# Down products of the middle pairs: weights standing and 512 tokens moving, output turned by VectorE

## The chip, the cores and the metric

The kernel runs on one core of one Trainium2 chip. The metric is the device time of one execution in microseconds (us). A core has TensorE for matrix products, VectorE and ScalarE for elementwise work, GpSimd, and SyncE, which here only issues DMAs. SBUF is the working memory with 128 partitions. Products go to PSUM, which has eight banks; a bank holds 512 float32 values on each of the 128 partitions. Each engine takes its instructions in the order in which the program gives them, and waits for other engines through semaphores.

## The reference

The program is a delta-rule attention followed by a dense layer pair.

- Attention: batch 4, 8 heads, 768 steps, head width 48. With normalized keys, step t gives `y[t] = q[t] @ state`, and then `state += beta[t] * outer(k[t], v[t] - k[t] @ state)`.
- The results of the heads stand beside each other: `x` has 3,072 tokens of 384 values.
- Dense part: `h = x @ w_in` (384 to 2,048); `g = h` where `h >= 1`, 0 where `h <= -1`, `(h + 1)^2 / 4` between; `out = g @ w_out` (2,048 to 384).

Inputs and output are float32.

## The kernel before, in words

The 768 steps are cut into 12 chunks of 64. Two chunks are a pair `G` (0 to 5); a pair has 512 tokens (4 batches, 2 chunks, 64 steps). For a pair, the dense part runs in 16 items, one for each 128 of the 2,048 middle columns (`items`, L614 to L621; pair 0 has its first columns split by chunk). While the dense items of pair G run, the attention of pair G+1 runs in pieces between them.

**An item.** `up` (L630) makes `h` (128 middle columns by 512 tokens) with nine products: three blocks of 128 rows of `x`, and three passes for each (`PASSES`: high part times high part, high times low, low times high, which together give float32 accuracy). ScalarE and VectorE make `g` from it (L776, L788, L789, maximum at L791), and `rest` (L753) splits it into `ghi` and `glo`, each a tile of 128 by 512 with two buffers. `down` (L639) multiplies `g` with `w_out`: for each of four blocks of 128 tokens, the tokens stand as weights and 384 columns of `WT` move, in three passes: twelve products an item. They accumulate over the 16 items in four banks, `o0` to `o3` (`oacc`, 128 tokens by 384). A down runs two items after its up (`LAG`), so the last down of pair G stands in item 1 of pair G+1, behind that item's up, and the first down of pair G+1 in item 2.

**The store.** After the last down of a pair, `store` (L653) copies the four banks to SBUF on ScalarE, and SyncE issues two DMAs for each bank, each of 64 tokens with 384 contiguous values. In the last pair ScalarE and VectorE take turns at the copies, and the very last DMA is issued by ScalarE.

**The order.** The schedule is written out by hand. Each item has two places for other work, at half-item numbers: `at(pe, G, t, ...)` puts a piece of products at item t of pair G (whole t: between up and down; half t: after down), and `at(fill, G, t, ...)` puts steps of other engines there. In the main loop (L765 to L794) an item gives, in this order: the late evictions of the piece before, `rest` of the item before, up, the first activation, the piece at t, the fills at t, the evictions of that piece, down and possibly store, two activations, the piece at t + 0.5, the maximum, the fills at t + 0.5. Pieces at half places are evicted at the start of the next item.

**The pieces of a pair** (`plan`, L674) for the chunks a and b of the next pair, in the middle pairs 1 to 4: `chain_r` 2.5, `gram_q(a)` 4.5, `gram_q(b)` 6, three merges (`merge32`, L385) at 8.5, 9 and 11, `gram_k` 9.5 and 12 (pairs 1 to 3), and the chain `chain_u`, `chain_y`, `chain_d`, `chain_r`, `chain_u`, `chain_y`, `chain_d` from 10 to 15. Each takes one or two banks from `acc()` (L65): from item 6 of pair 0 on, this is the name `ch` with two buffers, taken in turn. So the banks are: two `h`, two `ch`, four `o`. `gram_q` is evicted by VectorE with three masked multiplications (L237), the merges by ScalarE (L399 to L406).

**The solve.** A triangular system for each pair is solved on VectorE in 30 steps of two instructions (L325, L327), spread by a cost sum over the items from 2.5 or 1.5 before a pair's start to its item 6 or so; then four steps turn the result (L333 to L338), which the merges read. The steps are fills, so they stand on VectorE's queue between the glo subtraction and the maximum of the items.

**DMA.** SyncE's queue is in order too: it holds the loads of keys, queries and values for later pairs (`load_k`, `load_q`, `load_kv`), the moves of `chain_y` (L484) and the stores. `load_kv(b + 2)` stands right behind a pair's stores.

Of the kernel before, what the change touches and what calls it, by code (L numbers as in the profile page):

```python
# [7 lines left out]
F32 = mybir.dt.float32  # L8
# [5 lines left out]
C = 64  # L14
NP = 4
D = 48
CT = 2
NV = CT * NP
DM = 384
# [11 lines left out]
def delta_rule_moe(ctx: ExitStack, tc: tile.TileContext, kqa, kqb, kv, beta, w, out):  # L31
# [185 lines left out]
    def gram_q(g):  # L217

        x, b_ = Q[g], banks(C)
        for j in range(H):  # L220
            for e, f in quarters():
                r, o = slice(f * C, f * C + D), other(e, f) * C
                nc.tensor.matmul(b_[e][o:o + C, j], K[g][r, e * H + j, :], x[r, (1 - f, 1)[e], e * H + j, :], start=True, stop=True)  # L223

        def moved():
            for o in range(2):
                yield x[o * C:o * C + C, o, 0:H], b_[0][o * C:o * C + C], slice(o * C, o * C + C)
            yield x[:, 0, H:NU], b_[1], slice(0, P)

        def evict():  # L230
            def raw():
                for a, b, r in moved():
                    nc.scalar.copy(out=a, in_=b)

            def masks(copied=False):
                for a, b, r in moved():
                    nc.vector.tensor_tensor(out=a, in0=a if copied else b, in1=mask[r, None, :].broadcast_to([r.stop - r.start, H, C]), op=ALU.mult)  # L237
                    yield
            return (raw, masks(True)) if g < 2 else lambda: run(masks())
        return evict  # L240
# [389 lines left out]
    def up(G, f, bs):  # L630
        h = ps.tile([P, 2 * NB], F32, name="h", bufs=2)
        n = 0
        for k in range(3):
            for x, y in PASSES:
                nc.tensor.matmul(h[:, cols(bs)], WT[f][:, 0, x, k * P:(k + 1) * P], XB[G][:, y, k, cols(bs)], start=(n == 0), stop=(n == 8))  # L635
                n += 1
        return h

    def down(G, f, bs):  # L639
        ghi, glo = gs.pop((G, f, bs))  # L640
        for b in bs:
            left[G, b] -= 1
            for k in (2 * b, 2 * b + 1):
                if (G, k) not in oacc:
                    oacc[G, k] = ps.tile([P, DM], F32, name=f"o{k}")
                    new = True
                else:
                    new = False
                for n, (x, y) in enumerate(PASSES):
                    nc.tensor.matmul(oacc[G, k], (ghi, glo)[x][:, k * P:(k + 1) * P], WT[f][:, 1, y, :],  # L650
                                     start=(new and n == 0), stop=(left[G, b] == 0 and n == 2))

    def store(G, b):  # L653
        o = sb.tile([P, 2, DM], F32, name="wx", bufs=2)
        for k in (2 * b, 2 * b + 1):
            (nc.scalar.copy, nc.vector.tensor_copy)[k % 2 if G == NS - 1 else 0](out=o[:, k % 2], in_=oacc[G, k])
            for j in range(CT):
                (nc.scalar if G == NS - 1 and k + j == TT else nc.sync).dma_start(out=out.rearrange("(b n t) m -> n b t m", b=CB, t=C)[2 * G + b, k % 2 * CT + j], in_=o[j * C:j * C + C, k % 2])

    pe, fill = {}, {}  # L660

    def at(where, G, t, *x):
        where.setdefault(2 * first[G] + int(round(2 * t)), []).extend(x)
# [5 lines left out]
    def chain(G, t, a):  # L669
        for j, f, g in ((0, chain_u, a), (0.5, chain_y, a), (1.5, chain_d, a), (2.5, chain_r, a + 1), (3.5, chain_u, a + 1), (4, chain_y, a + 1), (5, chain_d, a + 1)):  # L670
            if (f, g) != (chain_d, ntot - 1):
                at(pe, G, t + j, lambda f=f, g=g: f(g))

    def plan(G):  # L674

        a, b = 2 * G + 2, 2 * G + 3
        if G == NS - 1:
            return
        va, vb = scale_v(a), scale_v(b)
        if G == 0:  # L680
            for j, f in ((0, merge16_b), (0.5, chain_r), (1, lambda g: merge32(g, None, True)), (2, lambda g: merge32(None, g)), (3, chain_u), (4, chain_y), (5, chain_d)):
                at(pe, G, j, lambda f=f: f(1))
            back = restore()
            at(fill, G, 0, (sv[1], 2))
            at(fill, G, 1, (load_k, b), (weight_loads, 7, 9), (load_q, a), (weight_loads, 9, 10), (load_kv, a), (weight_loads, 10, 13))
            at(fill, G, 1.5, (back, 1))
            at(fill, G, 2.5, (back, 1), (raws[1][1], 9))
            for j, n in enumerate((2, 2, 3)):
                at(fill, G, 3.5 + j, (early[0], n))
            at(fill, G, 6.5, (early[1], 1))  # L690
            at(fill, G, 7, (early[1], 9))
            at(fill, G, 4.5, (load_q, b), (weight_loads, 13, 14))
            at(fill, G, 5.5, (load_kv, b), (weight_loads, 14, 15))
            at(fill, G, 8, (load_k, a + 2), (weight_loads, 15, FT))
            for j in range(2):
                at(fill, G, 6 + j / 2, (va, 1))
                at(fill, G, 11.5 + j / 2, (vb, 1))
            at(pe, G, 6, lambda: gram_q(a))
            at(pe, G, 7, lambda: chain_r(a))
            at(pe, G, 11, lambda: gram_q(b))  # L700
            for j, f in ((8, merge16_a), (9.5, merge16_b)):
                for g in range(2):
                    at(pe, G, j + g / 2, lambda f=f, g=g: f(g))
            M = 12.5
            last = FT + HALF
        else:
            so, un = solves.pop(G)
            at(fill, G, 0.5, (va, 1))
            at(fill, G, 1, (va, 1))
            at(pe, G, 2.5, lambda: chain_r(a))  # L710
            at(pe, G, 4.5, lambda: gram_q(a))
            at(pe, G, 6, lambda: gram_q(b))
            cost, hs = 0, 0
            t, n = (-2.5, 19) if G == 1 else (-1.5, 17)
            for j in range(1, 31):
                at(fill, G, t + hs / 2, (so, 1))
                cost += j * (31 - j) + 150
                hs = int(cost / 9461 * n)
            for j, t in enumerate((7, 7.5, 8, 8)):
                at(fill, G, t, (un, 1))  # L720
            at(fill, G, 9, (vb, 1))
            at(fill, G, 9.5, (vb, 1))
            M = 8.5
            last = 16
        for j, x in ((0, (0, None)), (0.5, (1, 0)), (2.5, (None, 1))):
            at(pe, G, M + j, lambda x=x: merge32(*x))
        chain(G, M + 1.5, a)
        if G < NS - 2:
            if G:
                at(fill, G, 6.5, (load_k, a + 2))  # L730
            at(fill, G, M + 0.5, (load_k, b + 2, (nc.sync, nc.sync), True))
            at(pe, G, M + 1, lambda: gram_k(a + 2))
            at(pe, G, M + 3.5, lambda: gram_k(b + 2))
            lane_steps(G, M + 2, lanes(G + 2), 2.5, 3, 3.5, 4)
            solves[G + 1] = solve_whole(), unlanes_whole()
            at(fill, G, M + 3, (load_q, a + 2))
            at(fill, G, M + 5, (load_k, b + 2))
            at(fill, G, M + 6.5, (load_q, b + 2))
            at(fill, G, last + 0.5, (load_kv, a + 2))
            at(fill, G, last + 1.5, (load_kv, b + 2))  # L740
# [24 lines left out]
    for n, item in enumerate(items):  # L765
        at_, c = 2 * n, cols(item[2])
        finish(late)
        if last:
            rest(*last)
            ready.append(last[0])  # L770
        if at_ == 2 * HALF:
            spare.clear()
        h = up(*item)

        s = sb.tile([P, 2 * NB], F32, name="s", bufs=2)
        relu(s[:, c], h[:, c], mid, -0.5)  # L776
        evicts = products(*pe.pop(at_, []))
        run(wu, 3 if n == 0 else 1)
        fills(at_)
        finish(evicts)  # L780
        run(wu, 2 if n < HALF else 1)
        if len(ready) == LAG:
            x = ready.pop(0)
            down(*x)
            for b in x[2]:
                if left[x[0], b] == 0:
                    store(x[0], b)
        relu(s[:, c], s[:, c], one, -1.0)  # L788
        nc.scalar.activation(out=s[:, c], in_=s[:, c], func=AF.Square)  # L789
        late = products(*pe.pop(at_ + 1, []))  # L790
        nc.vector.tensor_tensor(out=s[:, c], in0=h[:, c], in1=s[:, c], op=ALU.max)  # L791
        run(wu, 2)
        fills(at_ + 1)
        last = item, s  # L794
# [3 lines left out]
    for b in range(2):  # L798
        gs[G, FT - 1, (b,)] = gs[G, FT - 1, (0, 1)]
        down(G, FT - 1, (b,))  # L800
        store(G, b)

# [1 line left out]
def layouts(q, k, v, beta, moe_w_in, moe_w_out):  # L804
# [43 lines left out]
```

## Time and profile before

| what | value |
|---|---|
| median of three runs | 622.01 us (621.1 to 622.45) |
| the profiled execution | 620.85 us |
| its span, first to last instruction | 619.1 us |
| mean granted TensorE clock | 0.943 |
| TensorE products busy | 583.6 us, 94% |
| VectorE busy | 409.3 us, 66% |
| ScalarE busy | 393.9 us, 64% |
| up products with 512 columns | 810, 402 ns mean |
| down products with 384 columns | 1,152, 339 to 344 ns mean |

The times of single products overlap, since TensorE is pipelined; how fast they follow each other is read from their starts. The rows of the profile have the start in us, the length, the engine (PE is TensorE, PEld its weight loads, DVE is VectorE, ACT is ScalarE, SPq the DMA queue of SyncE), the line, the operation, the tiles written and read, the shape and the count, and in brackets the idle time before it with what ended it.

### The profile page before, as it was taken

How to read it: one execution, taken by the hardware profiler on the slowest of the kernel's cores; microseconds unless marked ns; L12 is line 12 of the kernel's file. 1: busy time of each engine (PE TensorE's matmuls, PEld its weight loads, DVE VectorE, ACT ScalarE, POOL GpSimd, SP SyncE). 2: the span in 40 equal slices, each digit the busy share in tenths (PEclk: the TensorE clock that was granted, in tenths of full speed). 3: DMA queues.
4: the chain of work that ended last, by engine and by line, in shares of the span. 5: the costliest groups of instructions: out<-in, count | busy, mean ns of one | idle time of the engine just before them, and what ended most of it. 6: DMA issues, size and time to landing. Idle time of an engine off the chain costs nothing.

```text
span 619.1 us, 21754 instructions
## 1 busy us (share of the span) xinstructions
PE 583.6 (94%) x9562; PEld 511.5 (83%) x9562; DVE 409.3 (66%) x848; ACT 393.9 (64%) x685; POOL 29.8 (5%) x62
## 2 busy tenths in 40 slices
PE   7977967799999999999999999999999999999996
PEld 7966956688888888888888888888888888889995
DVE  4989899972379873379973489954489945333332
ACT  3436775649667569656578646587647586666663
POOL 5110000010010000020000020000020000000000
PEclk9556697999999999999999999999999999999999
DMA  5672756200124210214210224110124000020002
GB/s 141 197 244 71 233 196 202 88 4 3 42 61 119 74 31 3 69 31 125 72 30 8 65 53 119 54 31 24 49 71 124 1 4 16 12 54 1 0 1 51
DMA packets 32831, 42.97 MB, mean 69 GB/s; under 512 B 7152, under 2 KB 27440, under 8 KB 32736
## 3 DMA queue, kind: packets, MB, share of 16 engines
q1 hardware_dynamic: 31600, 39.43, 22.6%
q10 hardware_dynamic: 880, 2.07, 1.0%
q8 instruction: 75, 1.23, 0.8%
q0 software_dynamic: 256, 0.08, 0.1%
q14 instruction: 20, 0.16, 0.1%
HBM read 34.47 MB, written 4.72 MB: 63 GB/s over the span
## 4 chain that ended last, share of the span: by engine, by line
PE 70%; ACT 11%; DVE 9%; SPq 3%; DMA 3%; issue 2%; DVEq 0%; ACTq 0%
PE o L650 27%; PE h L635 27%; PE ch L452 3%; ACT XT L406 2%; ACT GG L404 2%; PE ch L414 2%; ACT s L762 2%; PE ch L223 2%; PE ch L430 1%; ACT XT L399 1%; PE ch L496 1%; PE o L583 1%; PE ch L375 1%; ACT s L789 1%; SPq L484 1%
## 5 line engine op out<-in xcount | busy, mean ns | idle before, releaser
L635 PE MATMUL h<-xb,wt 128*128 128x512 f32 (+1 forms) x918 | 229.1, 395 | 9.1 <-DMA xb<-wt 8.1
L635 PEld LDWEIGHTS h<-xb,wt 128*128 128x128 f32 x918 | 166.8, 195 | 43.2 <-DVE xb L183 4.4
L650 PE MATMUL o<-wt,ghi 128*128 128x384 f32 x768 | 202.1, 344 | 0.1
L791 DVE TENSOR_TENSOR s<-h,s 128x512 f32<-128x512 f32 (+1 forms) x102 | 66.8, 655 | 124.3 <-ACT s L789 123.8
L650 PEld LDWEIGHTS o<-wt,ghi 128*128 128x128 f32 x768 | 137.8, 189 | 7.5 <-issue 0.5
L757 ACT CAST ghi<-s 128x512 fp32r<-128x512 f32 (+1 forms) x102 | 60.8, 597 | 110.4 <-DVE s L791 86.3
L650 PE MATMUL o<-wt,glo 128*128 128x384 f32 x384 | 130.3, 339 | 0.4 <-DVE glo L758 0.3
L762 ACT ACTIVATE s<-h,half 128x512 f32<-128x512 f32 (+1 forms) x102 | 67.5, 662 | 44.6 <-PE h L635 43.7
L758 DVE TENSOR_TENSOR glo<-s,ghi 128x512 fp32r<-128x512 f32 (+1 forms) x102 | 66.6, 653 | 34.9 <-ACT ghi L757 34.8
L650 PEld LDWEIGHTS o<-wt,glo 128*128 128x128 f32 x384 | 72.7, 189 | 1.0 <-DVE glo L758 1.0
L762 ACT ACTIVATE s<-s,one 128x512 f32<-128x512 f32 (+1 forms) x102 | 71.7, 703 | 2.4
L789 ACT ACTIVATE s<-s 128x512 f32<-128x512 f32 (+1 forms) x102 | 61.9, 607 | 3.2
L325 DVE TENSOR_TENSOR pr<-A 128x30 f32<-128x30 f32 (+14 forms) x120 | 39.3, 328 | 6.2 <-POOL A L296 4.5
L327 DVE TENSOR_TENSOR A<-A,pr 128x30 f32<-128x30 f32 (+14 forms) x120 | 39.9, 332 | 4.4
L452 PEld LDWEIGHTS ch<-Q,SU 64*64 64x64 f32 (+1 forms) x1008 | 22.1, 135 | 4.3 <-ACT ghi L757 1.5
L452 PE MATMUL ch<-Q,SU 64*64 64x64 f32 (+1 forms) x1008 | 24.3, 222 | 0.7 <-ACT SU L434 0.7
L237 DVE TENSOR_TENSOR Q<-ch,mask 64x512 f32<-64x512 f32 (+1 forms) x30 | 20.6, 688 | 0.4
L296 POOL TENSOR_SCALAR_AFFINE_SELECT A<-A 128x1024 f32<-128x1024 f32 x4 | 5.1, 1263 | 311.9 <-DMA xb<-X 258.1
L404 ACT ACTIVATE GG<-ch 32x512 f32<-32x512 f32 x22 | 13.0, 589 | 10.6 <-PE ch L392 10.3
L414 PEld LDWEIGHTS ch<-SU,K 48*64 48x64 f32 x672 | 13.2, 147 | 6.5 <-issue 4.6
L414 PE MATMUL ch<-SU,K 48*64 48x48 f32 x672 | 14.9, 232 | 3.7 <-DVE Q L237 3.7
L179 ACT ACTIVATE xb<-wt 128x768 f32<-128x768 f32 x16 | 14.5, 914 | 5.1 <-DVE wt L191 3.6
(150 smaller groups left out, 621.8 us busy)
## 6 DMA issues: line engine op xcount, KB each, us to landing
wt<-in_w_dram SPq DMA_DIRECT2D x14, 768.0 KB, 5.4
out_dram<-wx SPq DMA_DIRECT2D x47, 96.0 KB, 2.2
KV<-in_kv_dram SPq DMA_DIRECT2D x36, 96.0 KB, 2.5
KV<-in_kv_dram SPq DMA_DIRECT2D x72, 48.0 KB, 2.4
KV<-in_kv_dram SPq DMA_DIRECT2D x12, 192.0 KB, 2.7
xb<-X SPq DMA_DIRECT2D x60, 32.0 KB, 2.0
K<-in_kqb_dram SPq DMA_DIRECT2D x12, 128.0 KB, 2.7
Q<-in_kqb_dram SPq DMA_DIRECT2D x12, 128.0 KB, 2.7
```

The costliest lines, as they stand in the source:

```text
L325: nc.vector.tensor_tensor(out=pr, in0=A[:, 0:n, j:j + 1].broadcast_to([P, n, m]), in1=A[:, j:j + 1, j + 1:32].broadcast_to([P, n, m]), op= ...
L327: nc.vector.tensor_tensor(out=A[:, 0:n, j + 1:32], in0=A[:, 0:n, j + 1:32], in1=pr, op=ALU.add)
L404: nc.scalar.mul(out=GG[r:r + 32, ga, :, 0:32], in_=y1[r:r + 32], mul=-1.0)
L414: nc.tensor.matmul(b_[f][o:o + C, j], K[g][r, k, :], SU[r, (1 - f, 1)[e], k, :], start=True, stop=True)
L452: nc.tensor.matmul(yy[i][o * C:o * C + C, e, p], SF[rows, u:u + C], w_[rows, x, k, :], **how)
L635: nc.tensor.matmul(h[:, cols(bs)], WT[f][:, 0, x, k * P:(k + 1) * P], XB[G][:, y, k, cols(bs)], start=(n == 0), stop=(n == 8))
L650: nc.tensor.matmul(oacc[G, k], (ghi, glo)[x][:, k * P:(k + 1) * P], WT[f][:, 1, y, :], start=(new and n == 0), stop=(left[G, b] == 0 and n ...
L757: nc.scalar.copy(out=ghi[:, c], in_=s[:, c])
L758: nc.vector.tensor_tensor(out=glo[:, c], in0=s[:, c], in1=ghi[:, c], op=ALU.subtract)
L762: nc.scalar.activation(out=out, in_=in_, func=AF.Relu, bias=bias, scale=scale)
L789: nc.scalar.activation(out=s[:, c], in_=s[:, c], func=AF.Square)
L791: nc.vector.tensor_tensor(out=s[:, c], in0=h[:, c], in1=s[:, c], op=ALU.max)
```

## The change

1. In pairs 1 to 4, `down_across` takes the place of `down`: the weights stand (`WT[f][:, 1, y, k::3]`, every third of 384 columns, 128 of them), and all 512 tokens of `ghi` or `glo` move. Nine products an item; the result has 128 output columns by 512 tokens in each of three banks, `o0` to `o2`. `k::3` gives bank k the columns k, k+3, and so on.
2. `store_across` turns it on VectorE: six transposes in blocks of 32 by 32, from 128x256 of PSUM to SBUF with a step of three elements, so that three banks interleave to rows of 96 contiguous values. Then SyncE issues 16 DMAs for each pair, each of 32 partitions with four runs of 96 values. ScalarE's four copies for each of these pairs go.
3. The bank `o3`, free in the middle pairs, becomes a third one for the pieces, from item 2 of pair 1 on.
4. In pairs 1 to 4, `gram_q(b)` moves from 6 to 8.5, behind the first merge there, and the third merge from 11 to 10.5, ahead of `chain_y`.
5. The last pair keeps `down`. Its stores are made by `store_last`: copies by ScalarE and VectorE in turn as before, the first half of each bank's tokens sent by SyncE, the second by ScalarE.

```diff
+    def down_across(G, f, bs):
+        g = gs.pop((G, f, bs))
+        for b in bs:
+            left[G, b] -= 1
+        for k in range(3):
+            if f == 0:
+                oacc[G, k] = ps.tile([P, 2 * NB], F32, name=f"o{k}")
+            for n, (x, y) in enumerate(PASSES):
+                nc.tensor.matmul(oacc[G, k], WT[f][:, 1, y, k::3], g[x],
+                                 start=(f == 0 and n == 0), stop=(f == FT - 1 and n == 2))
+
+    def store_across(G):
+        o = [sb.tile([P, CT, TT, 32, 3], F32, name="wx", bufs=2) for _ in range(2)]
+        for k in range(3):
+            for x in range(2):
+                nc.vector.transpose(out=o[x][:, :, :, :, k].rearrange("p e (b h) d -> p b e h d", b=2),
+                                    in_=oacc[G, k].rearrange("p (b x n) -> p x b n", b=2, x=2)[:, x].rearrange("p b (e h d) -> p b e h d", e=CT, h=2))
+        for x in range(2):
+            for e in range(CT):
+                for i in range(4):
+                    nc.sync.dma_start(out=out.rearrange("(e n t) (i m) -> e i t n m", e=CB, t=32, i=4)[2 * x + e, i, :, 4 * G:4 * G + 4],
+                                      in_=o[x][32 * i:32 * i + 32, e].rearrange("p n d k -> p n (d k)"))
+
     def store(G, b):
         o = sb.tile([P, 2, DM], F32, name="wx", bufs=2)
         for k in (2 * b, 2 * b + 1):
-            (nc.scalar.copy, nc.vector.tensor_copy)[k % 2 if G == NS - 1 else 0](out=o[:, k % 2], in_=oacc[G, k])
+            nc.scalar.copy(out=o[:, k % 2], in_=oacc[G, k])
             for j in range(CT):
-                (nc.scalar if G == NS - 1 and k + j == TT else nc.sync).dma_start(out=out.rearrange("(b n t) m -> n b t m", b=CB, t=C)[2 * G + b, k % 2 * CT + j], in_=o[j * C:j * C + C, k % 2])
+                send(G, k, j, o, nc.sync)
+
+    def send(G, k, j, o, q):
+        q.dma_start(out=out.rearrange("(b n t) m -> n b t m", b=CB, t=C)[2 * G + k // 2, k % 2 * CT + j], in_=o[j * C:j * C + C, k % 2])
+
+    def store_last(G):
+        o = [sb.tile([P, 2, DM], F32, name="wx", bufs=2) for _ in range(2)]
+        for k in range(TT + 1):
+            if k < TT:
+                (nc.scalar.copy, nc.vector.tensor_copy)[k % 2](out=o[k // 2][:, k % 2], in_=oacc[G, k])
+                send(G, k, 0, o[k // 2], nc.sync)
+            for x in ((0,), (), (1,), (), (2, 3))[k]:
+                send(G, x, 1, o[x // 2], nc.scalar)
...
-            at(pe, G, 6, lambda: gram_q(b))
...
-        for j, x in ((0, (0, None)), (0.5, (1, 0)), (2.5, (None, 1))):
+        for j, x in ((0, (0, None)), (0.5, (1, 0)), (2 if G else 2.5, (None, 1))):
             at(pe, G, M + j, lambda x=x: merge32(*x))
+        if G:
+            at(pe, G, M, lambda: gram_q(b))
...
+        if item[:2] == (1, 2):
+            spare[:] = START[0:2] + [dict(name="o3", bufs=1)]
         h = up(*item)
...
             x = ready.pop(0)
-            down(*x)
-            for b in x[2]:
-                if left[x[0], b] == 0:
-                    store(x[0], b)
+            if 0 < x[0] < NS - 1:
+                down_across(*x)
+                if x[1] == FT - 1:
+                    store_across(x[0])
+            else:
+                down(*x)
+                for b in x[2]:
+                    if left[x[0], b] == 0:
+                        store(x[0], b)
...
         down(G, FT - 1, (b,))
-        store(G, b)
+    store_last(G)
```

## The prediction

> **What bounds the kernel now.** I read first the busy shares and the chain of waits, then each middle pair as one stretch.
>
> ```profile
> PE 583.6 (94%) x9562; PEld 511.5 (83%) x9562; DVE 409.3 (66%) x848; ACT 393.9 (64%) x685; POOL 29.8 (5%) x62
> ...
> PE 70%; ACT 11%; DVE 9%; SPq 3%; DMA 3%; issue 2%; DVEq 0%; ACTq 0%
> ```
>
> ```profile
> 284.84:374.42 89.58, 89.32 (x1425) 77.55 (x1425) 62.19 (x138) 59.60 (x104) 3.50 (x6) 1.00 0.22 57
> ...
> 380.00:390.00 10.00, 10.00 (x108) 8.86 (x108) 9.61 (x24) 6.54 (x11) 0.00 (x0) 1.00 0.40 110
> ```
>
> The columns are the stretch, its length, the busy time of TensorE, its weight loads, VectorE, ScalarE and GpSimd, and then the granted clock. The first stretch is pair 2, from its third up to that of pair 3: TensorE has no gap worth the name, at full clock (1.00), so only TensorE time counts there. The second lies in the stretch where the triangular solve runs: VectorE is busy 9.61 of 10 us. The average of 66% hides that. The wait view for VectorE says the same: in 44 us it waited once.
>
> ```profile
> DVE s L791 <- ACT s L789: 0.3, 1, 0.3
> ```
>
> That is the whole answer for 366 to 410 us. So there are two full engines from the end of one pair to the middle of the next, and whatever VectorE is given there comes later by as much.
>
> **The products.** How long a product takes is read from starts, since ends are modelled.
>
> ```profile
> 184.19 1.23 PE L635 MATMUL h<-xb,wt 128*128 128x256 f32 x9
> 185.26 0.52 PE L650 MATMUL o<-wt,ghi 128*128 128x384 f32 x2
> ...
> 562.62 2.22 PE L635 MATMUL h<-xb,wt 128*128 128x512 f32 x9
> 564.68 0.51 PE L650 MATMUL o<-wt,ghi 128*128 128x384 f32 x2
> ...
> 566.76 2.25 PE L635 MATMUL h<-xb,wt 128*128 128x512 f32 x9
> 568.85 0.51 PE L650 MATMUL o<-wt,ghi 128*128 128x384 f32 x2
> ```
>
> Nine products with 512 columns moving take 564.68 - 562.62 = 2.06 us, and 2.09 the next time: 0.231 us each. The twelve of a down take 566.76 - 564.68 = 2.08: 0.173 each. Both move 4,608 columns, and pay per column. The new down has the shape of an up, so I expect 9 x 0.231 = 2.08 us where 2.08 stood. Over 64 downs (4 pairs of 16): **0**, with the spread of the two ups, 0.02 us, either way as bounds: 1.3 us of gain or of loss.
>
> One thing is new in it: the weight load reads every third column. Nine products of 256 columns took 185.26 - 184.19 = 1.07 us, 0.119 each, so a load of contiguous weights takes at most 0.119 and lies under 0.231. No row shows a strided one. The nearest are VectorE's transposes:
>
> ```profile
> L282 DVE STREAM_TRANSPOSE A<-GG 128x1024 f32<-128x1024 f32 x5 | 10.0, 1999 | 0.0
> L338 DVE STREAM_TRANSPOSE GG<-XT 128x512 f32<-128x512 f32 x8 | 5.2, 689 | 0.0
> L333 DVE TENSOR_TENSOR A<-A,gm 128x1024 f32<-128x1024 f32 x4 | 4.9, 1218 | 0.0
> L352 DVE STREAM_TRANSPOSE XT<-A 128x512 f32<-128x512 f32 x2 | 2.0, 998 | 0.0
> L791 DVE TENSOR_TENSOR s<-h,s 128x256 f32<-128x256 f32 x12 | 5.0, 420 | 6.1 <-ACT s L789 6.0
> ```
>
> Reading with a step of 64 elements made 1024 elements cost 1999 instead of 1218 ns, 1.64 times. A load 1.64 times as long is 0.195 us: still hidden. So nothing is charged; twice is a rival below.
>
> [...]
>
> **Turning the output.** Six transposes of 128x256 for each pair, PSUM to SBUF, writing with a step of three elements, take the place of four copies on ScalarE. By the rows above a transpose with runs of 32 costs what an elementwise operation costs (689 for 512, between 420 for 256 and 1218 for 1024), so 256 elements cost 0.42 us; one that writes with a step of 64 costs 998 against 689, 0.31 more for 512, so 0.58 for 256 at the worst. I take the middle, **0.5**. The question is where they stand in VectorE's order.
>
> ```profile
> 374.42 2.26 PE L635 MATMUL h<-xb,wt 128*128 128x512 f32 x9
> 376.52 0.52 PE L650 MATMUL o<-wt,ghi 128*128 128x384 f32 x2
> ...
> 378.74 1.15 PE L414 MATMUL ch<-SU,K 48*64 48x48 f32 x64
> ```
>
> ```profile
> 375.19 1.61 ACT L656 COPY wx<-o 128x384 f32<-128x384 f32 x4
> ...
> 377.42 0.40 DVE L327 TENSOR_TENSOR A<-A,pr 128x228 f32<-128x228 f32 x1
> 378.12 0.69 DVE L791 TENSOR_TENSOR s<-h,s 128x512 f32<-128x512 f32 x1 [0.30 <-ACT s L789]
> ...
> 467.71 0.69 DVE L791 TENSOR_TENSOR s<-h,s 128x512 f32<-128x512 f32 x1 [0.31 <-ACT s L789]
> ```
>
> This is the passage from pair 2 to pair 3. Pair 2's last down ends at 374.42, where the up of item 2 of pair 3 starts. ScalarE copies the accumulators from 375.19 on, four in 1.61 us, and at 376.52 the first down of pair 3 starts in the same banks, 1.3 us after the first copy began. In the new order the transposes stand on VectorE behind the fills of that item, that is behind a scaling of KV and two solve steps, the last of which ends at 377.8, and ahead of the maximum of 378.12. Banks come free two transposes at a time: at 378.8, 379.8 and 380.8 with 0.5 us each. The down of pair 3 writes banks 0, 1 and 2 in this order, so its last three products start at 380.8 and end at 380.8 + 3 x 0.231 = 381.5, instead of 378.6 (the 376.52 and 2.08). TensorE is in order: behind it wait a chain piece and the next up. **Stall: 6 x 0.5 - 0.1 = 2.9 us**, 2.4 at 0.42 and 3.4 at 0.58. The passage from pair 3 to 4 shows the same row at 467.71, with the same 0.3 us behind a full VectorE, and that from 1 to 2 looks the same, so 3 x 2.9 = **8.7 us** (7.2 to 10.2). The passage from pair 0 keeps the old store. From pair 4 to 5 no solve runs:
>
> ```profile
> 548.75 1.98 ACT L656 COPY wx<-o 128x384 f32<-128x384 f32 x4
> 552.04 0.69 DVE L791 TENSOR_TENSOR s<-h,s 128x512 f32<-128x512 f32 x1 [3.80 <-ACT s L789]
> ```
>
> VectorE stands idle 3.80 us there, longer than 6 x 0.5, while TensorE runs an up: nothing. ScalarE's 1.6 us per pair saved is worth 0 at these places, it isn't late there.
>
> The stores become 16 issues on SP for each pair instead of 8. Eight took 5.01 us and the KV loads come behind them:
>
> ```profile
> 375.69 5.01 SPq L658 DMA_DIRECT2D out_dram<-wx  x8
> ```
>
> Sixteen take 10 us, from about 381 on, so those loads come some 10 us later. The scaling that reads them stands at items 9 and 9.5, eight items of over 4.1 us (the up and the down) later, and the work of these items hides it: 0; without that cover it would cost up to the 10.
>
> **The pieces and the third bank.** A piece alone on TensorE pays for changing over and back.
>
> ```profile
> 340.40 1.15 PE L496 MATMUL ch<-SU,KV 64*48 64x48 f32 x64
> 341.48 2.38 PE L635 MATMUL h<-xb,wt 128*128 128x512 f32 x9
> ...
> 343.79 1.16 PE L210 MATMUL ch<-A 48*64 48x64 f32 x64
> ```
>
> From 341.48 to 343.79 the up takes 2.31 instead of 2.08: 0.2 us for each place. Two merges now stand beside another piece, in four pairs: 8 x 0.2 = **1.6 us** gained (0 if changing between pieces costs as much). The moved gram_q takes its own 1.1 us along, and its three masks of 512 elements (0.69 us each, by 420 ns for 256 and 1218 for 1024) leave VectorE's full stretch for the stretch after the solve, where VectorE is idle; this makes up for 2.1 of the 3.0 us of transposes there, so the merge behind the solve isn't late by VectorE: TensorE, already 2.9 late, comes later still.
>
> With `o3` as a third bank the waits for a bank behind the merges should go:
>
> ```profile
> 324.92 0.33 PE L210 MATMUL ch<-K 48*64 48x64 f32 x2
> 325.42 1.16 PE L210 MATMUL ch<-K 48*64 48x64 f32 x62 [0.17 <-ACT GG L404]
> ...
> 328.79 1.54 PE L430 MATMUL ch<-KV,XT 64*64 64x48 f32 x64
> ...
> 510.21 2.28 PE L452 MATMUL ch<-Q,SU 112*64 112x64 f32 x96 [0.66 <-ACT SU L434]
> ```
>
> gram_k's two first products wait 0.5 us for their bank, chain_u takes 1.54 instead of 1.15: 0.9 in each of three pairs. In pair 4 chain_y waits 0.66, which a merge ahead of it covers. At most 3 x 0.9 + 0.66 = 3.4; ScalarE runs without a gap through this stretch and allows perhaps three quarters: **2.5 us** (0 to 3.4).
>
> **The last stores.**
>
> ```profile
> 612.16 4.40 SPq L658 DMA_DIRECT2D out_dram<-wx  x7
> ...
> 613.22 0.56 DVE L656 COPY wx<-o 128x384 f32<-128x384 f32 x1 [0.48 <-PE o L650]
> 613.81 0.56 ACTq L658 DMA_DIRECT2D out_dram<-wx  x1
> ```
>
> Seven issues on SP end at 616.56, 0.63 each, and the span at 619.1, 2.5 later. With four on each queue ScalarE's come last: one between its copies, one after the second copy (about 613.2), then two, so 613.2 + 3 x 0.56 = 614.9 and 617.4 with the same 2.5: **1.7 us** (1.2 to 2.2).
>
> **Sum.** 8.7 - 1.6 - 2.5 - 1.7 = 2.9 us slower. The profiled execution took 620.85 us (span 619.1 and 1.75 around it), so 623.75; the median of the timed runs is 622.01, 1.16 above, and the forecast against it **624.9 us**. The bounds of the terms together: best 7.2 - 1.6 - 3.4 - 2.2 - 1.3 = -1.3, worst 10.2 - 1.2 + 1.3 = +10.3.
>
> **Rivals.** (1) *No stall at the passages*: VectorE reaches the transposes before TensorE needs the banks. The fills ahead of them would have to end at 378.6 - 0.7 - 3.0 = 374.9, where now they end at 377.8; against it speak three equal passages and no idle time on VectorE. If so, only gains are left: 622.0 - 5.8 = 616.2 us, faster. Chance 0.22. Half of it, with transposes near 0.3 us (no row has this), gives about 620 to 622, no change: with the low end of the forecast's own bounds 0.15. (2) *The strided load binds*: the load at twice the 0.119 is 0.238 against 0.231, so 9 x 0.007 x 64 = 4 us more, 629; it decides from 1.9 times on, and each further tenth of a time costs 9 x 0.012 x 64 = 6.9 us. For it speaks 1.64 on another engine; against it that 12 bytes is a small step. Chance 0.10. (3) *The clock falls in the stalls*:
>
> ```profile
> 88.00:90.00 2.00, 0.00 (x0) 0.00 (x0) 2.00 (x4) 0.56 (x2) 0.00 (x0) 1.00 0.17 42
> 90.00:92.00 2.00, 1.38 (x4) 0.74 (x4) 1.89 (x5) 1.97 (x5) 0.00 (x0) 0.74 0.24 53
> 92.00:94.00 2.00, 2.00 (x5) 1.46 (x6) 1.96 (x5) 0.58 (x1) 0.00 (x0) 0.50 0.45 129
> ...
> 110.00:112.00 2.00, 0.00 (x0) 0.00 (x0) 2.00 (x3) 0.00 (x0) 0.00 (x0) 1.00 0.84 347
> ```
>
> After the idle stretch around 88 to 90 the clock fell to 0.74 and 0.50, worth 2 x (0.26 + 0.50) = 1.5 us; after that of 110 to 112 it stayed 1.00. The new stall is 2.3 us and then two short ones, nearer the second. If it fell three times: 624.9 + 4.5 = 629.4. Chance 0.08.
>
> **Numbers.** Forecast 0.45, rivals as above. What differs by under 0.2% (1.24 us) can't be told from no change. Faster: rival 1 and a little of the forecast's low end, 0.25; same 0.17; slower 0.58. The forecast's own range is 621 to 632; with the faster rival the range is 616 to 631.
>
> **What would show it.** A wait of TensorE before o for a VectorE transpose, 2 to 3 us, three times, none at the passage to pair 5; transposes of 0.42 to 0.58 us; an up and a new down both 2.08 us; weight loads that stay under 0.231; no wait of chain_u; the span ending some 4 us after the last product instead of 5.9. If the first down of pairs 2 to 4 starts without a gap, the forecast is wrong; if the new downs take over 2.1 us, rival 2 is at work.

## The result, and the profile after

The changed kernel takes 626.42 us (median of 6 runs, 624.26 to 627.81) where the kernel before takes 622.23 (6 runs): 1.0062 of before, 95% interval 1.0038 to 1.0085. In later runs (`after_again` below) it took 625.90 us beside 621.71: 1.0078, interval 1.0060 to 1.0097. It is 4 to 5 us slower; the forecast was 2.9 us slower. The profiled execution took 627.81 us, with a span of 626.1 at a mean granted clock of 0.934.

First the busy shares and the shares of the chain of waits, in the order of the prediction.

```profile
PE 586.5 (94%) x9370; PEld 513.7 (82%) x9370; DVE 418.8 (67%) x872; ACT 389.5 (62%) x669; POOL 29.8 (5%) x62
...
PE 70%; DVE 15%; ACT 5%; SPq 3%; DMA 3%; issue 3%; POOL 0%; POOLq 0%; DVEq 0%; ACTq 0%
```

TensorE's share is the same, but VectorE's share of the chain rose from 9 to 15% and ScalarE's fell from 11 to 5%. Where VectorE is on the chain, the waits of TensorE say (the columns are the total in us, how often, and the longest); the stretch is 200 to 620 us:

```profile
PE o L661 <- DVE wx L668: 6.1, 3, 2.1
```

No other wait of TensorE shows there: three waits of about 2 us, before the new down product, for the transposes. The passage from pair 1 to pair 2 in time order (start, length, engine, line; the wait before an instruction in square brackets):

```profile
284.70 2.26 PE L635 MATMUL h<-xb,wt 128*128 128x512 f32 x9
...
287.72 0.40 DVE L327 TENSOR_TENSOR A<-A,pr 128x228 f32<-128x228 f32 x1
288.03 2.27 DVE L668 STREAM_TRANSPOSE wx<-o 128x256 f32<-128x256 f32 x6
...
289.04 0.77 PE L661 MATMUL o<-ghi,wt 128*128 128x512 f32 x2 [2.07 <-DVE wx L668]
...
289.88 0.63 PE L661 MATMUL o<-ghi,wt 128*128 128x512 f32 x2
...
290.18 0.64 DVE L834 TENSOR_TENSOR s<-h,s 128x512 f32<-128x512 f32 x1
...
290.64 1.05 PE L661 MATMUL o<-ghi,wt 128*128 128x512 f32 x2
...
381.72 0.77 PE L661 MATMUL o<-ghi,wt 128*128 128x512 f32 x2 [2.00 <-DVE wx L668]
...
474.44 1.00 PE L661 MATMUL o<-ghi,wt 128*128 128x512 f32 x2 [2.07 <-DVE wx L668]
```

The mechanism is as predicted: the transposes stand behind the solve's steps, start at 288.03, and TensorE waits from 286.97 (289.04 less 2.07), when its up is done. The size is another. Six transposes take 2.27 us together, 0.38 each, though one alone reads 473 ns in the groups below: they overlap. After the first two the first bank is free, and the second and third come free in time: the products on them (289.88 and 290.64) have no wait. So only the first two transposes are waited for, not six.

The products after the wait are slow: the last of the down take 1.05 us where two of them took 0.63. The windows say why (length, busy times of TensorE, its weight loads, VectorE, ScalarE and GpSimd, then the granted clock, DMA share, GB/s):

```profile
284.70:377.47 92.77, 90.70 (x1377) 78.47 (x1376) 64.75 (x144) 58.64 (x100) 3.52 (x6) 0.98 0.20 54
...
287.07:290.49 3.42, 1.45 (x6) 1.40 (x7) 3.35 (x10) 0.00 (x0) 0.00 (x0) 1.00 0.00 0
290.49:293.90 3.41, 3.41 (x69) 2.62 (x67) 3.27 (x9) 2.56 (x4) 0.00 (x0) 0.50 0.45 100
382.65:386.06 3.41, 3.41 (x39) 2.40 (x41) 3.31 (x8) 2.40 (x4) 0.00 (x0) 0.50 0.35 80
474.81:478.22 3.41, 3.41 (x9) 2.34 (x8) 3.34 (x9) 1.88 (x3) 0.00 (x0) 0.50 0.27 61
```

In the 3.42 us from 287.07 TensorE is busy for 1.45, at full clock; the next 3.41 us run at half. The other two waits are followed by 3.41 us at half as well. The first row is pair 2, from its third up to that of pair 3: 92.77 us where it took 89.58 before. The whole budget, with starts read in the same way in both traces:

| stretch | before, us | after, us | difference |
|---|---|---|---|
| start to item 2 of pair 1 | 195.29 | 195.89 | +0.60 |
| pair 1 | 89.55 | 88.81 | -0.74 |
| pair 2 | 89.58 | 92.77 | +3.19 |
| pair 3 | 89.55 | 92.65 | +3.10 |
| pair 4 | 86.08 | 88.67 | +2.59 |
| item 2 of pair 5 to the end | 69.05 | 67.31 | -1.74 |
| sum | 619.1 | 626.1 | +7.0 |

The first row lies ahead of everything that the change touches; its 0.6 us differ from run to run (195.3 to 198.1 us in the profiles of this document). The profiled run was the slowest of its six.

The groups of the new lines (busy us, mean ns of one, idle time before):

```profile
L661 PE MATMUL o<-ghi,wt 128*128 128x512 f32 x384 | 126.6, 411 | 6.1 <-DVE wx L668 6.1
L661 PEld LDWEIGHTS o<-ghi,wt 128*128 128x128 f32 x384 | 92.4, 254 | 10.9 <-issue 7.4
...
L668 DVE STREAM_TRANSPOSE wx<-o 128x256 f32<-128x256 f32 x24 | 9.1, 473 | 0.6 <-PE o L661 0.6
```

In the kernel before:

```profile
L650 PEld LDWEIGHTS o<-wt,ghi 128*128 128x128 f32 x768 | 137.8, 189 | 7.5 <-issue 0.5
```

A weight load that reads every third column takes 254 ns; the contiguous one of before took 189. And the end:

```profile
620.62 2.51 SPq L684 DMA_DIRECT2D out_dram<-wx  x4
...
621.31 0.34 PE L650 MATMUL o<-wt,glo 128*128 128x384 f32 x1
...
621.55 1.90 ACTq L684 DMA_DIRECT2D out_dram<-wx  x3
```

The last product before:

```profile
612.84 0.34 PE L650 MATMUL o<-wt,glo 128*128 128x384 f32 x1
```

From the start of the last product (621.31) to the end of the span it is 4.79 us; before it was 619.1 - 612.84 = 6.26. The stores from two queues bring 1.5.

### The profile page after: what moved, and what is told of

Same layout as the page of the kernel before. It is cut to its first block, busy times and chain, and to the rows that moved or that the text cites. A ratio compares the mean times of both kernels' runs of the same rounds, so it can differ in the third digit from the quotient of the medians.

```text
span 626.1 us, 21405 instructions
## 1 busy us (share of the span) xinstructions
PE 586.5 (94%) x9370; PEld 513.7 (82%) x9370; DVE 418.8 (67%) x872; ACT 389.5 (62%) x669; POOL 29.8 (5%) x62
## 3 DMA queue, kind: packets, MB, share of 16 engines
q10 hardware_dynamic: 1120, 2.36, 1.2%
q8 instruction: 74, 1.21, 0.8%
## 4 chain that ended last, share of the span: by engine, by line
PE 70%; DVE 15%; ACT 5%; SPq 3%; DMA 3%; issue 3%; POOL 0%; POOLq 0%; DVEq 0%; ACTq 0%
PE h L635 26%; PE o L661 20%; PE o L650 8%; PE ch L452 2%; DVE SU L511 2%; DVE pr L325 1%; PE ch L414 1%; DVE A L327 1%; DVE glo L794 1%; PE o L583 1%; DVE s L834 1%; PE ch L375 1%; PE ch L392 1%; PE ch L430 1%; DMA K<-in_kqb_dram 1%
## 5 line engine op out<-in xcount | busy, mean ns | idle before, releaser
L661 PE MATMUL o<-ghi,wt 128*128 128x512 f32 x384 | 126.6, 411 | 6.1 <-DVE wx L668 6.1
L661 PEld LDWEIGHTS o<-ghi,wt 128*128 128x128 f32 x384 | 92.4, 254 | 10.9 <-issue 7.4
L661 PE MATMUL o<-glo,wt 128*128 128x512 f32 x192 | 77.5, 404 | 0.0
L650 PE MATMUL o<-wt,ghi 128*128 128x384 f32 x256 | 68.6, 349 | 0.1
L661 PEld LDWEIGHTS o<-glo,wt 128*128 128x128 f32 x192 | 48.7, 254 | 0.4
L650 PEld LDWEIGHTS o<-wt,ghi 128*128 128x128 f32 x256 | 46.5, 192 | 2.8 <-issue 0.5
L650 PE MATMUL o<-wt,glo 128*128 128x384 f32 x128 | 44.1, 344 | 0.3 <-DVE glo L794 0.3
L650 PEld LDWEIGHTS o<-wt,glo 128*128 128x128 f32 x128 | 24.6, 192 | 0.8 <-DVE glo L794 0.8
L452 PE MATMUL ch<-Q,SU 64*64 64x64 f32 (+3 forms) x768 | 21.9, 222 | 0.0
L452 PEld LDWEIGHTS ch<-Q,SU 64*64 64x64 f32 (+3 forms) x768 | 19.7, 135 | 1.8 <-ACT ghi L793 0.7
```

Source lines behind the costliest of these rows:

```text
L452: nc.tensor.matmul(yy[i][o * C:o * C + C, e, p], SF[rows, u:u + C], w_[rows, x, k, :], **how)
L661: nc.tensor.matmul(oacc[G, k], WT[f][:, 1, y, k::3], g[x], start=(f == 0 and n == 0), stop=(f == FT - 1 and n == 2))
```

## The experiments

Eleven runs follow, on three chips, each beside the kernel before on the same chip (medians 621.54, 621.71 and 621.81 us). The theory is that the loss is the place of the transposes in VectorE's order; the first rival, that VectorE is full there, so that any place only moves the loss.

**The transposes ahead of the fills** (`early`).

```diff
+        full = len(ready) == LAG
+        if full and 0 < ready[0][0] < NS - 1 and ready[0][1] == FT - 1:
+            x = ready.pop(0)
+            down_across(*x)
+            store_across(x[0])
+            full = False
...
         run(wu, 2 if n < HALF else 1)
-        if len(ready) == LAG:
+        if full:
             x = ready.pop(0)
             if 0 < x[0] < NS - 1:
                 down_across(*x)
-                if x[1] == FT - 1:
-                    store_across(x[0])
```

> The changed kernel with one move: in the item that holds a middle pair's last down, that down and the six transposes are given out ahead of the item's fills, so on VectorE the transposes stand before the scaling of KV and the solve steps. Theory S (the cost of the change is the wait at three passages, 2.1 to 2.3 us each, and the half clock that follows it for 3.2 us, 1.6 us each): the wait before the first new down shrinks to under 0.3 us, the clock stays 1.00, and of the 11.5 us some 8 come back, since VectorE, with the same work, is ready for the merge only about 1 us before TensorE asks for it now: about 618 us, faster than before. Theory F (VectorE is full, so its 2.3 us of transposes come out of the time wherever they stand): the wait moves to the first merge behind the solve, at least 2 us there in each of three pairs; only the clock's share comes back: about 622 us, no change against before. Theory L (the strided weight load is the cost): nothing changes, 626 us.

Measured: 618.43 us, 0.9948 of before (0.9930 to 0.9967). The same kernel on the other two chips:

> The same kernel as the run named early, for the comparison on this chip: 618.4 us (0.995 of before).

> The same kernel as the run named early, beside the two runs without one of its parts, on one chip: 0.995 to 0.996 of before, 618.4 to 619.4 us.

Measured: 619.38 us, 0.9961 (0.9947 to 0.9975), and 618.85 us, 0.9955 (0.9939 to 0.9971). This version beats both kernels. Its passage, in time order:

```profile
285.11 2.26 PE L635 MATMUL h<-xb,wt 128*128 128x512 f32 x9
...
285.91 2.29 DVE L668 STREAM_TRANSPOSE wx<-o 128x256 f32<-128x256 f32 x6
...
287.21 0.63 PE L661 MATMUL o<-ghi,wt 128*128 128x512 f32 x2
...
289.77 0.40 DVE L327 TENSOR_TENSOR A<-A,pr 128x228 f32<-128x228 f32 x1
290.08 0.68 DVE L838 TENSOR_TENSOR s<-h,s 128x512 f32<-128x512 f32 x1
```

The longest of its waits of TensorE in the stretch from 200 us on, and pair 2's window:

```profile
PE h L635 <- DVE s L838: 0.6, 2, 0.4
```

```profile
285.11:374.82 89.71, 89.08 (x1377) 77.66 (x1376) 64.48 (x143) 58.12 (x100) 3.51 (x6) 1.00 0.23 59
```

The transposes start 0.80 us after the up (285.91), where they started 3.33 us after it in the changed kernel; they run under the up. The down follows at 287.21 without a gap, and the clock stays at 1.00. VectorE does the same work as in the changed kernel, in another order; its maximum comes 4.97 us after the up, where it came 5.48 after it there, and TensorE waits only 0.6 us for it in this whole stretch. So the loss is not given back: the first rival falls.

**Products in the wait** (`busy`). Nine more products, whose result is thrown away, stand ahead of the first down of pairs 2 to 4, so that TensorE is not idle there.

```diff
         for k in range(3):
             if f == 0:
                 oacc[G, k] = ps.tile([P, 2 * NB], F32, name=f"o{k}")
...
+        if f == 0 and G > 1:
+            idle = ps.tile([P, 2 * NB], F32, **acc())
+            for _ in range(9):
+                nc.tensor.matmul(idle, WT[f][:, 1, 0, 0:P], g[0], start=True, stop=True)
```

> The changed kernel with nine more products in the first down of pairs 2, 3 and 4, ahead of it: contiguous weights and 512 tokens into a bank of the pieces that nobody reads, 2.08 us of TensorE work where it now waits 2.1 to 2.3 us for the transposes. They add work that is thrown away; the output is unchanged. Theory S: the wait itself stays, filled, so it costs no time, but TensorE isn't idle, the clock stays 1.00, and up to 1.6 us come back at each passage where the clock falls: 3 to 5 us, about 622 to 623. If the clock doesn't fall because of the idle time, or the wait isn't what costs: no gain, and up to 3 x 2.08 us more, 626 to 632.

Measured: 623.96 us, 1.0039 of before (1.0026 to 1.0053), 1 us above what was expected if the clock counts. The waiting view has no row for the transposes any more, and the windows over the first passage show TensorE busy and the clock whole:

```profile
286.00:289.00 3.00, 3.00 (x14) 2.40 (x14) 2.90 (x8) 1.22 (x2) 0.00 (x0) 1.00 0.12 32
289.00:292.00 3.00, 3.00 (x36) 2.40 (x36) 2.96 (x9) 0.83 (x2) 0.00 (x0) 1.00 0.15 33
```

Against 1.0062 and 1.0078 that is 1.4 to 2.4 us better, with as much TensorE time taken as the waits took. So the falling clock costs about 2 us of the timed runs, less than the three falls in the profiled run of the changed kernel would.

**The changed kernel again** (`after_again`), on one chip with the second `early`.

> The changed kernel itself, beside the others on one chip: 1.004 to 1.008 of before, 624 to 627 us. If the clock falls at all three passages in the profile again, its loss is near 5 us and the time near 627; if at none, near 623.5 (the waits without the clock).

Measured: 625.90 us, 1.0078. Its profile shows the same three waits, shorter by up to 0.5 us, and only one fall:

```profile
288.87 0.77 PE L661 MATMUL o<-ghi,wt 128*128 128x512 f32 x2 [1.88 <-DVE wx L668]
...
380.07 0.77 PE L661 MATMUL o<-ghi,wt 128*128 128x512 f32 x2 [1.52 <-DVE wx L668]
...
471.31 0.77 PE L661 MATMUL o<-ghi,wt 128*128 128x512 f32 x2 [2.07 <-DVE wx L668]
```

```profile
290.00:292.00 2.00, 2.00 (x58) 1.65 (x60) 1.97 (x5) 1.22 (x3) 0.00 (x0) 1.00 0.33 74
...
382.00:384.00 2.00, 2.00 (x69) 1.60 (x68) 1.93 (x5) 1.94 (x4) 0.00 (x0) 1.00 0.51 114
...
472.00:474.00 2.00, 2.00 (x8) 1.59 (x6) 1.96 (x6) 0.81 (x2) 0.00 (x0) 0.68 0.22 49
```

With `early` as the kernel without the wait, what a passage costs can now be read pair by pair (the mean of the three profiles of `early` for pairs 2, 3, 4: 90.07, 88.98, 85.62 us):

| profile | pair | wait, us | clock fell | stretch less that of `early`, us |
|---|---|---|---|---|
| after | 2 | 2.07 | yes | 2.70 |
| after | 3 | 2.00 | yes | 3.67 |
| after | 4 | 2.07 | yes | 3.05 |
| after_again | 2 | 1.88 | no | 1.49 |
| after_again | 3 | 1.52 | no | 1.71 |
| after_again | 4 | 2.07 | yes | 3.06 |

A wait costs 1.6 us, a fall 1.5 more (3.1 less 1.6). That is two passages against four, and the two waits without a fall were the shorter ones (1.70 us on the mean against 2.05), so a part of the 1.5 may be the wait's. In the timed runs the difference between the changed kernel and `early` is 1.0062 - 0.9948 and 1.0078 - 0.9961, 7.1 and 7.3 us, 2.4 for each passage: with 1.6 for the wait, the clock falls about every second time. This is worked out, since only the profiled runs show the clock along their length.

**The pieces and the bank as before** (`old_pieces`): the change with the products' and the stores' parts alone.

```diff
+            at(pe, G, 6, lambda: gram_q(b))
...
-        for j, x in ((0, (0, None)), (0.5, (1, 0)), (2 if G else 2.5, (None, 1))):
+        for j, x in ((0, (0, None)), (0.5, (1, 0)), (2.5, (None, 1))):
...
-        if G:
-            at(pe, G, M, lambda: gram_q(b))
...
-        if item[:2] == (1, 2):
-            spare[:] = START[0:2] + [dict(name="o3", bufs=1)]
```

> The changed kernel with the pieces where they stood: the second gram_q at item 6, the third merge at 11, and no third bank for the pieces. New downs, transposes and last stores stay. Theory S: the pieces and the bank are worth about 1.3 us in each of four pairs (pair 1, which has no wait, came out 0.74 us shorter although its new downs cost about 0.6 more), so about 5 us more: 631 to 632. If they were worth nothing: 626. Theory F adds that the masks of gram_q, 2.1 us, are back in VectorE's full stretch and each of three pairs waits for them at the merge: 636 or more.

Measured: 629.27 us, 1.0119 of before (1.0092 to 1.0145). Against 1.0062 and 1.0078 the pieces and the bank together are worth 3.5 and 2.5 us, where about 5 was expected. In its profile the clock fell at none of its passages, while the changed kernel's falls at about half; that hides a part. Its waits were

```profile
292.31 0.77 PE L661 MATMUL o<-ghi,wt 128*128 128x512 f32 x2 [1.45 <-DVE wx L668]
...
384.58 0.77 PE L661 MATMUL o<-ghi,wt 128*128 128x512 f32 x2 [1.21 <-DVE wx L668]
...
477.20 0.77 PE L661 MATMUL o<-ghi,wt 128*128 128x512 f32 x2 [2.08 <-DVE wx L668]
```

Pair by pair against `after_again` its four stretches are longer by 1.46, 0.95, 1.06 and -0.40 us; the last one has the fall of the other in it, so 1.1 without its 1.5. That makes some 4.6 us.

**The bank and the places apart**, each taken away from `early`, where no wait at a passage disturbs.

```diff
--- early_nobank
-        if item[:2] == (1, 2):
-            spare[:] = START[0:2] + [dict(name="o3", bufs=1)]
--- early_nomove
+            at(pe, G, 6, lambda: gram_q(b))
...
-        for j, x in ((0, (0, None)), (0.5, (1, 0)), (2 if G else 2.5, (None, 1))):
+        for j, x in ((0, (0, None)), (0.5, (1, 0)), (2.5, (None, 1))):
...
-        if G:
-            at(pe, G, M, lambda: gram_q(b))
```

> The run named early without the third bank for the pieces, so that the bank's worth is seen without any wait at the passages. My step put the bank at 2.5 us (0 to 3.4): 621 us, with gram_k's wait of 0.5 us back three times and chain_u at 1.5 instead of 1.1 us. Rival, that once two merges stand beside other pieces the two banks would do: 618.5 us.

> The run named early with gram_q(b) and the third merge at their old places (the third bank stays). My step put the two joined places at 1.6 us (0 to 1.6), 0.2 us for each of eight: 620 us, 1.6 above early. Rival, that a change from piece to piece costs TensorE as much as one from a piece to a large product: 618.5 us.

Measured: without the bank 633.40 us, 1.0187 of before (1.0163 to 1.0211); with the old places 623.43 us, 1.0033 (1.0016 to 1.0049). `early` on the same chip is at 0.9955, so the bank is worth 14.4 us and the places 4.9: both expectations, mine and the rivals', missed. The waits of TensorE without the bank:

```profile
PE ch L223 <- ACT GG L404: 4.1, 4, 1.0
PE ch L452 <- ACT XT L399: 3.9, 4, 1.0
```

and with the old places:

```profile
PE ch L392 <- DVE XT L335: 0.8, 2, 0.4
PE o L392 <- DVE XT L335: 0.4, 1, 0.4
```

Without the bank each joined place waits 1.0 us until ScalarE has emptied the merge's banks: gram_q behind the first merge, chain_y behind the third, in four pairs, 8.0 us; the clock fell twice besides (around 232 and 526 us). What is left of the 14.4 has no single row. With the old places the merges wait 1.2 us for the solve's last steps (L335), because gram_q(b)'s masks and the transposes both stand in VectorE's full stretch (the kernel before has the masks there and `early` the transposes, and neither has such a wait); the other 3.7 us have no row of their own; that these are the changes of the eight pieces that stand alone again is argued, not shown.

**The weights' layout.** `contig` takes the 128 weights side by side in the changed kernel, which leaves the output columns of pairs 1 to 4 in another order. `early_cols` does it in `early` with the columns of `w_out` laid out in that order from the start, so that the output is the same.

```diff
-                nc.tensor.matmul(oacc[G, k], WT[f][:, 1, y, k::3], g[x],
+                nc.tensor.matmul(oacc[G, k], WT[f][:, 1, y, k * P:(k + 1) * P], g[x],
```

> The changed kernel with contiguous weights in the new downs: 128 neighbouring columns of w_out instead of every third. The same products in number and size; the output columns of pairs 1 to 4 land in another order, so the output isn't the reference's. Theory S, with a small cost of the load: loads fall from 254 to about 189 ns, a new down between two ups from 2.10 to 2.08 us, one behind a small piece from 2.36 to 2.29, so 64 x 0.02 + 16 x 0.07 = 2.4 us back: about 624. Theory L: the load is the main cost, 4 us or more come back, to 622 or less. If the load is hidden altogether: 626.

> The last down of a middle pair and its transposes stand ahead of the item's fills (as in the run named early), and the columns of w_out are laid out so that the 128 weights of each load lie side by side; the output is the same. Theory that the strided load costs only behind small pieces: the load goes back from 254 to about 190 ns, a new down behind a piece takes 2.30 instead of 2.36 us, and the time is 1 to 1.5 us under that of early, some 617 us (0.992 to 0.993 of before). Rival, that the load's stride cost nothing and the other layout's 1.5 us came from fewer falls of the clock: the same time as early, 618.4 us, with the clock at 1.00 in both.

Measured: `contig` 623.95 us, 1.0035 (1.0016 to 1.0054); `early_cols` 618.41 us, 0.9960 (0.9939 to 0.9980) where `early` on the same chip has 0.9961. The second pair settles that the layout makes no difference that the times show. The rows of a down behind gram_k, of `early` and then of `early_cols` (in each the next row begins what follows it):

```profile
323.08 0.80 PE L661 MATMUL o<-ghi,wt 128*128 128x512 f32 x2
...
325.44 0.33 PE L210 MATMUL ch<-K 48*64 48x64 f32 x2
```

```profile
324.57 0.74 PE L661 MATMUL o<-ghi,wt 128*128 128x512 f32 x2
...
326.87 0.33 PE L210 MATMUL ch<-K 48*64 48x64 f32 x2
```

The down takes 2.36 us with the stride and 2.30 without. Over the 18 downs behind a small piece, at 0.06 to 0.07 each, that is 1.2 us; the four stretches together differ by 0.6 (353.72 and 353.13). Both are below what the times can tell. `contig`'s gain over the changed kernel cannot be put on the layout: it was not run beside the changed kernel on one chip, its waits were 1.66, 2.06 and 2.05 us, and its clock fell at two of three passages.

**The last stores alone** (`tail`): the kernel before with `store_last` only.

```diff
-        store(G, b)
+    store_last(G)
```

> The kernel before with only the last stores from two queues. My step put it at 1.7 us (1.2 to 2.2); the two traces at 1.5. Expected 620 us (0.9975 of before), span ending 4.8 us after the start of the last product. Rival, that the 1.5 us belong to the new last banks and not to the queues: no change, 621.5 us.

Measured: 619.65 us, 0.9981 of before (0.9969 to 0.9994), 1.2 us (0.4 to 1.9). The rows of its end; the span ends at 620.1:

```profile
614.54 2.39 SPq L661 DMA_DIRECT2D out_dram<-wx  x4
...
615.22 0.34 PE L650 MATMUL o<-wt,glo 128*128 128x384 f32 x1
...
615.31 1.93 ACTq L661 DMA_DIRECT2D out_dram<-wx  x3
```

4.9 us from the last product to the end, as in the changed kernel: it is the queues, not the banks.

## Why the prediction was right, and where it was not

The sign and nearly the size were right: 624.9 us was put, 626.42 and 625.90 came. The mechanism at the passages was right as well. That the number came so near is in part luck: the loss at the passages came out 1.5 us smaller than put and the gains 2.6 to 3.4 us smaller (5.8 put; `early`, which has them without the loss, gains 2.4 to 3.2), and the two errors work against each other. By its steps:

- **The passages** (8.7 us put): the place, how many there are and the cause were right. The terms were not. The stall was put at 2.9 us, six transposes at 0.5 waited for one after the other; it is a wait of 2.0 to 2.1 us, costing 1.6, since transposes follow each other at 0.38 and only the first two are waited for; the step took the duration of one as the pace of six, and let the last products wait for all of them. The clock's fall, rival 3, was put at 1.5 us and a chance of 0.08: about 1.5 us it is, and it happens at about half of the passages. The two errors cancel in part: 3 x 2.4 = 7.2 us by the timed runs, where 8.7 stood.
- **No stall at the passage to pair 5**: right, the view of waits counts three stalls and not four.
- **Rival 1** ("no stall") is not what the changed kernel does, but it is what `early` does. It was put at 616.2 us; `early` takes 618.4 to 619.4. The 2 to 3 us between are the terms that were put too well, below.
- **The products** (0, up to 1.3 either way): a new down between two ups takes 2.10 to 2.11 us where 2.08 stood. Taken for all 64 downs, though only 25 stand between two ups, that is an estimated 64 x 0.02 = 1.3 us lost, the end of the bounds. It is not the stride's: in `early_cols` the same downs take 2.10 to 2.12 (one 2.17).
- **The strided load** (0): the load rose from 189 to 254 ns, 1.34 times where 1.64 was reckoned with and 1.9 allowed. The prediction's own sign, a load under 0.231 us, fails, and downs over 2.1 us were to show rival 2 at work; both signs mislead. Loads overlap each other: even the 254 ns ones follow the pace of 0.234 between two ups, as the contiguous ones do. So where a product of 512 columns goes ahead the stride costs nothing that shows (2.10 to 2.11 us for a down with it, 2.10 to 2.12 without). Behind a small piece it shows, 0.06 to 0.07 us for a down, 1.2 us by the rows, which the times do not show. The step left out the 18 downs that stand behind small pieces.
- **The pieces and the bank** (-1.6 and -2.5): the sum of 4.1 was about right, 2.5 to 3.5 us by the times and 4.6 by the stretches. The split was wrong. The step priced each edit alone, from rows of the old order; but two merges beside other pieces need the third bank. With the places and without the bank it is 14.4 us slower than with both.
- **The relief of VectorE by gram_q's move** was right in kind: with the old places the merges wait for the solve, 1.2 us.
- **The last stores** (-1.7): -1.5 in the trace, -1.2 in the run alone, at the low end of 1.2 to 2.2.
- **SP's sixteen issues** (0): no wait of TensorE for a load of KV appeared.

By these, without the passages: -4.6 for the pieces and the bank, -1.5 for the stores, +1.3 and +1.2 for the products makes -3.6 us; the three runs of `early` gave -2.4 to -3.2. With 7.2 for the passages it is +3.6, where 3.9 and 4.9 were measured. About 1 us stays without a row (0.3 and 1.3).

## What to carry to other kernels

When work moves from an engine with slack to one without, its place in that engine's order can decide more than its price: the same six transposes cost 7 us behind the solve's steps and nothing that a wait shows ahead of them. A short wait of TensorE should be priced with the clock's possible fall behind it, here 1.6 and 1.5 us. Edits that share a resource, like places that need a bank, are priced together, since each alone can come out with the wrong sign.

## What was not expected of the hardware

- **The clock fell after waits of 2.00 to 2.07 us, and it went by where the wait lay on steps of 3.41 us.** In the profiles, waits at these passages of 1.21, 1.45, 1.52, 1.66 and 1.88 us left the clock at 1.00; those of 2.00, 2.05, 2.06 and three of 2.07 were followed by 3.41 us at 0.50. One of 2.08 (the last of `old_pieces`) was not, so the length alone does not decide. Within one profile all changes of the clock lie whole steps of 3.413 us apart: the falls at 290.49, 382.65 and 474.81 of the changed kernel are 27 steps from each other, and each lasts one step. Laid along these steps, the twelve passages of the four profiles with waits fall apart: a step that held 1.96 to 2.07 us of the wait was followed by a fall, six times of six, and one that held 1.70 or less was not, six times of six. The wait of 2.08 has 0.38 us in one step and 1.70 in the next:

```profile
475.50:478.91 3.41, 1.71 (x7) 1.66 (x8) 3.38 (x9) 0.00 (x0) 0.00 (x0) 1.00 0.00 0
478.91:482.33 3.42, 3.42 (x75) 2.78 (x74) 3.28 (x9) 2.56 (x4) 0.00 (x0) 1.00 0.47 104
```

The gap of the kernel before at 110 to 112 us, which the prediction took as its example without a fall, lies over such an edge too (111.43, one step behind the rise of its clock at 108.02): of its 2.32 us, 1.59 lie ahead of the edge and 0.73 behind it. A wait of 2.05 us laid anywhere on steps of 3.41 would hold 1.96 in one step in 45% of the places and 1.70 in 60%, an estimate that goes with the "every second time" above. Among small products less was enough: the two falls of `early_nobank` came after steps with only 1.02 and 1.36 us without a product. What sets the steps, and where between 1.70 and 1.96 us the border lies at these passages, no run shows.

- **Transposes overlap.** One of 128x256 from PSUM, writing with a step of three, reads 473 ns; six in a row take 2.27 us, 0.38 each. The prediction took a single duration for the pace of a row of them.
- **A weight load with a step of 12 bytes** takes 254 ns against 189, and costs nothing that shows behind products of 512 columns (2.10 to 2.11 us for a down with it, 2.10 to 2.12 without).
